# Attention feeding two MLP layers on one core: the opening's loads in another order, and two attention pairs per TensorE visit

## The chip, the core and the metric

The kernel runs on one core of a Trainium2 chip. Its engines each follow their own stream of instructions: TensorE (PE; its weight loads are listed as PEld), VectorE (DVE), ScalarE (ACT), GpSimd (POOL) and SyncE (SP), which here issues every DMA. The metric is the device time of one execution in microseconds (us); less is better.

## The reference

Attention over chunks of 32 tokens, each with 16 tokens before it, 8 after it and 8 memory tokens, for 4 batches of 768 tokens with 8 heads of 64; then two MLP layers on the 3072 tokens (512 to 2048 to 512 features each). All data are float32.

```
for c in range(nc):
    q_c = q[:, :, c_start:c_end]
    k_full = concat([mem_k, k[:, :, l_start:r_end]]);  v_full = concat([mem_v, v[:, :, l_start:r_end]])
    scores = scale * matmul(q_c, k_full.T)
    a = exp(scores - max(scores));  a = a / (sum(a) + 1e-09)
    out[:, :, c_start:c_end] = matmul(a, v_full)
x = out, tokens by features
h = x @ w_in;   x = maximum(0.01 * h, h) @ w_out              # layer 0
h = x @ w_in2;  x = (h * clip(h + 3, 0, 6) / 6) @ w_out2      # layer 1
```

## The kernel before

**Tiling.** The attention is done in 48 pairs of chunks (64 tokens, 8 heads, 96 context columns). A block is 512 tokens, so 8 pairs (`NPB`); there are 6 blocks (`NB`). Each layer goes through its 6 blocks, and a block through 16 steps f (`NF`, 128 hidden features each). A step has a hidden half and an output half (`hidden`, `output`), 12 products of 128x128 by 128x512 each: every operand is split into a high and a low part, and three of the four combinations are multiplied (`mm3`, L567). So the MLPs take 2 x 6 x 16 x 24 = 4608 such products. Between the two halves of a step, ACT applies the activation (L586), ACT writes its high part `gh` (L600) and DVE the low part `gl` (L609).

**Weights.** They arrive as float64 words (`w_load`, L211, 512 KB for one key, a key being one half of one step) in one of four `raw` buffers, and are turned into the high and low parts once per layer by ACT (L217, L223, L251) and DVE (clip L227, shift L231, join L238, add L245, low part L257). The `raw` buffer is free after L257. Layer 0's 32 keys are converted before and during block 0.

**Attention of one pair.** PE computes scores (`a_scores`, L326); in blocks 0 and 1 PE also adds the chunk mask for most pairs (L317), and DVE takes the maximum straight from PSUM (L356), POOL scales it (L367), ACT takes the exponentials, one per head pair with a sum (L402). For the pairs in `SHIFTED`, DVE subtracts the maximum (L375), ACT does one exponential (L387) and DVE adds up (L391). Other pairs are masked on DVE (L336, L362). Then POOL adds a small constant (L414), DVE inverts (L418), POOL normalises (L422). The probabilities are turned by PE (L440, copied by ACT L445) in blocks 0 and 1, by DVE (L432) after that. PE multiplies them with v (`a_values`, L453), and ACT and DVE split the result into the high and low parts of x (L468, L474).

**Order.** The order in which instructions are issued is not that of the loops. `Program` collects every piece of work as a step: engine, estimated length (`TIME`), a due time, the steps that it must follow, and the ring buffers that it takes and frees. `Program.order` then plays a list schedule: whenever an engine is free it takes, of the steps that are ready and whose ring has room, the one due first. Where PE has nothing ready before the opening's last turn, it puts in `keep_warm` (L659), two products of zeros. The instructions are issued in that order for good.

**The opening** is block 0's attention: all 8 pairs must be done before layer 0's first hidden half (due at `BEGIN`). The q and k of its pairs and their v are loaded into buffers of their own. `before = [values_done[x] for x in [pr - 3] if x >= 0]` makes a pair's scores follow the values of the pair three earlier, and a v load follows the q and k load of its pair. **Afterwards** pair pr of blocks 1 to 5 is scored while the block before is in the MLP: PE breaks off its products for a visit (`visit`, `visit_step`), which computes the scores of pair pr and the values of pair pr - 1; the values go into the upper part of the second score bank, `pa1`. q and k of these pairs share one buffer `qk_now`, v one buffer `v_now`. The hidden halves use a ring of two PSUM banks, `ph`.

Of the kernel before, what the change touches and what calls it, by code (L numbers as in the profile page):

```python
# [22 lines left out]
    words=0.67, clip=0.42, shift=0.43, join=0.69, add=0.69, high=0.65, low=0.69, load=0.47,  # L23
    visit=1.2, scores=0.75, masked=0.56, most=0.55, exp=1.65, exp_all=0.52, small=0.15, inverse=0.18, norm=0.83, turn=0.6, turned=0.57, turn4=0.95,
    values=0.85, xh=0.4, xl=0.45, half=1.36, act=0.58, six=0.69, gh=0.6, gl=0.69, done=0.66, warm=0.22,
# [6 lines left out]
STEP_FIRST, STEP_MIXED, STEP = 7.0, 6.6, 5.5  # L32
PAIR_FIRST = 2.1
SHIFTED = (2, 4, 6)


class Program:
# [15 lines left out]
    def order(self, filler):  # L53
# [81 lines left out]
def tile_kernel(  # L135
# [147 lines left out]


    def inputs(pr):
        if pr >= NPB:
            t, vt = qk_t, v_t
        else:
            if pr not in in_t:
                in_t[pr] = sb.tile([P, 2 * 2 * 512], F32, tag="w", name=f"in{pr}", bufs=NF)  # L290
            t, n = in_t[pr], HP * (PT + W)
            t, vt = t[:, :n], t[:W, n:n + HD]
# [3 lines left out]
    def load_qk(pr):  # L296
        nc.sync.dma_start(out=inputs(pr)[0], in_=qk[divmod(pr, PPB)])

    def load_v(pr):
        nc.sync.dma_start(out=inputs(pr)[3], in_=v[divmod(pr, PPB)])  # L300

# [68 lines left out]
    def a_shift(pr):  # L370
        e = sb.tile([P, HP, W], F32, tag="ye", name=f"e{pr}", bufs=4)
        mx = m_t.pop(pr)
        for j in range(2):
# [19 lines left out]

    def a_exp(pr):
        direct = barred_by_pe(pr)
        if direct:
            e_t[pr] = sb.tile([P, HP, W], F32, tag="ye", name=f"e{pr}", bufs=4)
        e, mx = e_t[pr], m_t.pop(pr)
        su = at.tile([P, HP], F32, tag="su", name=f"su{pr}", bufs=4)
        for hp in range(HP):  # L400
            j, m = divmod(hp, HP // 2)
            nc.scalar.activation(  # L402
                out=e[:, hp, :],
                in_=p_t[pr][j][:, m * W:(m + 1) * W] if direct else e[:, hp, :],
                func=AF.Exp,
                scale=SCALE if direct else 1.0,
                bias=mx[:, hp:hp + 1],
                accum_out=su[:, hp:hp + 1],
            )
        s_t[pr] = su  # L410

# [35 lines left out]

    def a_values(pr, pt):
        t, vt = aT_t.pop(pr), inputs(pr)[3]
        for hp in range(HP):  # L450
            for e in range(2):
                c, n = slice(hp * P + e * D, hp * P + (e + 1) * D), e ^ 2 * hp // HP
                nc.tensor.matmul(  # L453
                    pt[e * D:(e + 1) * D, hp * PT:(hp + 1) * PT], vt[:, c], t[:, hp, n * PT:(n + 1) * PT],
                    start=True, stop=True, tile_position=(0, e * D),
                )
# [5 lines left out]
    def a_xh(pr):  # L462
        blk, i = divmod(pr, NPB)
        if (0, blk) not in x_t:
            x_t[0, blk] = tuple(
                sb.tile([P, KD, TB], FR, tag=f"x{c}", name=f"x{c}{blk}", bufs=2) for c in "hl"
            )
        nc.scalar.copy(out=x_t[0, blk][0][:, :, i * PT:(i + 1) * PT], in_=px_t[pr])  # L468

    def a_xl(pr):  # L470
        blk, i = divmod(pr, NPB)
        xh, xl = x_t[0, blk]
        c = slice(i * PT, (i + 1) * PT)
        nc.vector.tensor_sub(out=xl[:, :, c], in0=px_t.pop(pr), in1=xh[:, :, c].bitcast(F32))  # L474
# [3 lines left out]
    def finish(pr, c, t, p):  # L478

        blk = pr // NPB  # L480
        first = pr % NPB == 0
        c = add("ACT", T["xh"], t + 0.8, a_xh, pr, after=[c] + ([] if first else x_ready[blk][:1]),
                takes=[("x", (0, blk))] if first else ())
        d = add("DVE", T["xl"], t + 1.3, a_xl, pr, after=[c], frees=p)
# [12 lines left out]
    def attention(pr, t, turned_by_pe, spread):  # L497

# [4 lines left out]

        qk, vv = [("qk", pr)], [("v", pr)]
        if blk == 0:
            qk = vv = [("w", ("in", pr))]
        hold = [] if blk == 0 else [scored[-3]] if pr == NPB else loaded[-1:]
        a = add("SP", T["load"], due(-5), load_qk, pr, after=hold, takes=qk, nbytes=P * 640 * 4)
        loaded.append(a)
        vl = add("SP", T["load"], due(0), load_v, pr, takes=vv if blk else (), after=[a], nbytes=W * 2048)  # L510
        s = [("py" if blk == 0 else f"pa{j}", ("s", pr, j)) for j in range(2)]
        e = [("ye", ("e", pr))]
        direct = barred_by_pe(pr)
        if blk == 0:
            before = [values_done[x] for x in [pr - 3] if x >= 0]
            c = add("PE", T["scores"] + 0.3 * direct, due(0), a_scores, pr, after=[a] + before + set_up, takes=s)
        else:
            c = visit_step(pr, t, [a], s, qk)
        scored.append(c)
        if direct:  # L520
# [6 lines left out]
            else:  # L527
                c = add("ACT", T["exp"], due(2.0), a_exp, pr, after=[c], takes=e, frees=s)
        else:
            c = add("DVE", T["masked"] + 0.06, due(1.1), a_masked, pr, after=[c] + set_up, takes=e, frees=s)  # L530
            c = add("DVE", T["most"], due(1.7), a_most, pr, after=[c])
            c = add("ACT", T["exp"], due(2.4), a_exp, pr, after=[c])
        c = add("POOL", T["small"], due(4.1), a_sums, pr, after=[c])
# [18 lines left out]
        else:  # L552
            pending[:] = [c, vl, aT + vv]

    def visit_step(pr, t, after=(), takes=(), frees=()):
        if not pending:
            return add("PE", T["scores"], t, visit, pr, after=[*after, opened[-1]], takes=takes, frees=frees)
        p = [*takes] or [("pa1", ("s", pr, 1))]
        c = add("PE", T["visit"], t, visit, pr, after=[*pending[:2], *after], takes=p,
                frees=pending[2] + [*frees])  # L560
        finish(pr - 1, c, t, p[-1:])
        return c
# [148 lines left out]
    for pr in range(NP):  # L711
# [131 lines left out]
```

## Time and profile before

| | |
|---|---|
| median of 3 runs | 1150.18 us (1149.99 to 1150.64) |
| the profiled execution | 1150.69 us, its span 1148.9 us |
| PE busy | 1139.2 us (99%), 6370 matmuls |
| DVE busy | 596.6 us (52%) |
| ACT busy | 467.3 us (41%) |
| POOL busy | 63.1 us (5%) |
| DMA | 78.65 MB, mean 68 GB/s |
| chain that ended last | PE 96%, DVE 2%, ACT 1% |

The profiled execution lies 0.5 us above the median, and 1.8 us of it lie outside the span. Shares are means over very different stages: the opening (to about 40 us), block 0 of layer 0 (to about 142 us) with the conversions, blocks 1 to 4 with visits (to about 533 us), and the rest, where PE does nothing but MLP products. Matmuls are pipelined, so that a PE shown as busy can still be issuing slower than it could; start times tell more than busy time.

### The profile page before, as it was taken

The page shows a single profiled execution, that of the slowest core. Times are in us where ns is not written, and L with a number is a line of the kernel's source. Part 1 is how long each engine was busy: PE and PEld are TensorE (multiplying, and loading weights), DVE is VectorE, ACT ScalarE, POOL GpSimd, SP SyncE. Part 2 cuts the span into 40 slices and gives each one's busy share as a digit, 9 for nine tenths or more (in the row PEclk, how much of TensorE's full clock was granted, in tenths as well). Part 3 has the DMA queues.
Part 4 walks back from the last instruction along what each step waited for, and adds up shares of the span by engine and source line. Part 5 has one row for each costly group of instructions (what it writes and reads, how often), then busy time and mean ns, then how long its engine had stood idle before and what let it go on. Part 6 is the DMA issues. An engine that isn't in the chain of part 4 may idle for free.

```text
span 1148.9 us, 16191 instructions
## 1 busy us (share of the span) xinstructions
PE 1139.2 (99%) x6370; PEld 927.4 (81%) x6370; DVE 596.6 (52%) x1299; ACT 467.3 (41%) x1052; POOL 63.1 (5%) x123
## 2 busy tenths in 40 slices
PE   9999999999999999999999999999999999999998
PEld 6777788888888888888888888888888888888887
DVE  5999985565555555564889723223223223222222
ACT  5888843333333333334777523223223223222222
POOL 3211110010010000100000000000000000000000
PEclk9999999999999999999999999999999999999999
DMA  8456521121111112113554202002002000000001
GB/s 257 142 190 195 184 92 38 55 74 38 56 46 65 56 37 74 57 37 103 179 162 168 92 1 74 1 1 74 1 1 73 1 1 35 3 1 24 14 1 37
DMA packets 31661, 78.65 MB, mean 68 GB/s; under 512 B 3424, under 2 KB 3424, under 8 KB 31584
## 3 DMA queue, kind: packets, MB, share of 16 engines
q1 hardware_dynamic: 31584, 77.61, 20.6%
q8 instruction: 50, 0.82, 0.3%
q14 instruction: 27, 0.22, 0.1%
HBM read 65.01 MB, written 12.58 MB: 68 GB/s over the span
## 4 chain that ended last, share of the span: by engine, by line
PE 96%; DVE 2%; ACT 1%; POOL 0%; issue 0%; DVEq 0%; POOLq 0%
PE py L567 46%; PE ph L567 45%; PE psc L453 2%; PE psc L326 2%; PE warm L659 1%; DVE wa L238 1%; DVE w L257 0%; ACT e L402 0%; PE pt L440 0%; DVE raw L245 0%; DVE wa L231 0%; DVE xl L474 0%; DVE mx L356 0%; DVE wa L227 0%; POOL su L414 0%
## 5 line engine op out<-in xcount | busy, mean ns | idle before, releaser
L567 PE MATMUL ph<-xh,w 128*128 128x512 f32 x768 | 253.1, 391 | 0.0
L567 PE MATMUL ph<-yh,w 128*128 128x512 f32 x768 | 252.0, 389 | 0.0
L567 PE MATMUL py<-gh,w 128*128 128x512 f32 x768 | 242.4, 396 | 0.5 <-DVE w L257 0.5
L567 PE MATMUL py<-w,gh 128*128 128x512 f32 x768 | 236.4, 389 | 0.0
L595 DVE SCALAR_TENSOR_TENSOR ph<-g,ph 128x512 f32<-128x512 f32 x96 | 66.8, 696 | 293.4 <-ACT g L589 293.4
L589 ACT ACTIVATE g<-ph,three 128x512 f32<-128x512 f32 x96 | 66.2, 690 | 297.6 <-PE ph L567 297.6
L567 PEld LDWEIGHTS ph<-xh,w 128*128 128x128 f32 x768 | 144.0, 188 | 30.9 <-DVE w L257 0.4
L567 PEld LDWEIGHTS py<-w,gh 128*128 128x128 f32 x768 | 144.2, 188 | 30.0
L567 PEld LDWEIGHTS ph<-yh,w 128*128 128x128 f32 x768 | 144.2, 188 | 29.8
L567 PEld LDWEIGHTS py<-gh,w 128*128 128x128 f32 x768 | 141.0, 188 | 31.0 <-DVE w L257 1.4
L567 PE MATMUL ph<-xl,w 128*128 128x512 f32 x384 | 149.5, 389 | 0.7 <-DVE xl L474 0.7
L567 PE MATMUL py<-gl,w 128*128 128x512 f32 x384 | 150.0, 391 | 0.0
L567 PE MATMUL py<-w,gl 128*128 128x512 f32 x384 | 149.4, 389 | 0.0
L567 PE MATMUL ph<-yl,w 128*128 128x512 f32 x384 | 149.4, 389 | 0.0
L432 DVE STREAM_TRANSPOSE aT<-e 32x128 f32<-32x128 f32 x384 | 116.0, 302 | 32.8 <-POOL e L422 27.4
L586 ACT ACTIVATE ph<-ph 128x512 f32<-128x512 f32 x96 | 55.9, 583 | 182.3 <-PE ph L567 182.2
L609 DVE TENSOR_TENSOR gl<-ph,gh 128x512 fp32r<-128x512 f32 x96 | 66.2, 690 | 59.6 <-ACT gh L600 58.5
L611 DVE SCALAR_TENSOR_TENSOR gl<-ph,gh 128x512 fp32r<-128x512 f32 x96 | 66.3, 691 | 56.3 <-ACT gh L602 56.1
L567 PEld LDWEIGHTS ph<-xl,w 128*128 128x128 f32 x384 | 72.1, 188 | 16.0 <-DVE xl L474 1.0
L567 PEld LDWEIGHTS py<-gl,w 128*128 128x128 f32 x384 | 72.0, 188 | 15.5
L567 PEld LDWEIGHTS ph<-yl,w 128*128 128x128 f32 x384 | 72.1, 188 | 15.0
L567 PEld LDWEIGHTS py<-w,gl 128*128 128x128 f32 x384 | 72.0, 188 | 15.0
(71 smaller groups left out, 933.3 us busy)
## 6 DMA issues: line engine op xcount, KB each, us to landing
raw<-in_moe_w_in_dram SPq DMA_DIRECT2D x32, 512.0 KB, 3.5
raw<-in_moe_w_out_dram SPq DMA_DIRECT2D x32, 512.0 KB, 3.8
qk_now<-in_qk_dram SPq DMA_DIRECT2D x40, 320.0 KB, 3.2
v_now<-in_v_dram SPq DMA_DIRECT2D x40, 192.0 KB, 2.6
y_dram<-yo SPq DMA_DIRECT2D x24, 256.0 KB, 2.0
yn<-y_dram SPq DMA_DIRECT2D x6, 1024.0 KB, 5.2
out_dram<-oo SPq DMA_DIRECT2D x24, 256.0 KB, 2.7
in<-in_qk_dram SPq DMA_DIRECT2D x8, 320.0 KB, 5.7
```

The costliest lines, as they stand in the source:

```text
L238: nc.vector.scalar_tensor_tensor(out=a, in0=hi, scalar=0xC0000000, in1=a, op0=ALU.bitwise_and, op1=ALU.bitwise_or)
L326: nc.tensor.matmul(pt[j][n * PT:(n + 1) * PT, m * W:(m + 1) * W], qt[r, hp, :], kt[r, hp, :], start=not more, stop=True, tile_position=(e ...
L432: nc.vector.transpose(out=t[c, :, r], in_=e[r, :, c])
L453: nc.tensor.matmul(pt[e * D:(e + 1) * D, hp * PT:(hp + 1) * PT], vt[:, c], t[:, hp, n * PT:(n + 1) * PT], start=True, stop=True, tile_posi ...
L567: nc.tensor.matmul(dst, a, b, start=first and i == 0, stop=last and i == len(terms) - 1)
L586: nc.scalar.activation(out=ph, in_=ph, func=AF.Prelu, alpha=0.01)
L589: nc.scalar.activation(out=g, in_=ph, func=AF.Relu, bias=three, scale=1.0)
L595: nc.vector.scalar_tensor_tensor(out=ph, in0=g, scalar=6.0, in1=ph, op0=ALU.min, op1=ALU.mult)
L609: nc.vector.tensor_sub(out=gl, in0=ph, in1=gh.bitcast(F32))
L611: nc.vector.scalar_tensor_tensor(out=gl, in0=ph, scalar=1.0 / 6.0, in1=gh.bitcast(F32), op0=ALU.mult, op1=ALU.subtract)
L659: nc.tensor.matmul(late["warm"][:, r], idle[:, :P], idle, start=True, stop=True)
```

## The change

In the opening, each pair's v load no longer follows its q and k load, and the first weight keys (f up to 2 of layer 0) are due 35 us instead of 9 us before their use, so that the order of the opening's loads is q and k of pair 0, weight key 0, q and k of pair 1, v of pair 0, and so on. A pair's scores follow the values of the pair five earlier instead of three. Pairs are due 1.9 us apart instead of 2.1. The pairs with a DVE shift are 3 and 5 instead of 2, 4 and 6. The planner counts `keep_warm` at twice its length until 5.5 us, so that fewer are put in at the start. A pair's four exponentials become four steps of the planner instead of one.

From pair 16 on (`doubled`), a visit computes the scores of pairs pr and pr + 1 (pr even) and the values of pairs pr - 2 and pr - 1; the second pair's scores stand in the upper part of the same two score banks, the values of both in a bank of the `ph` ring, and one copy of each kind splits both results. q, k and v of the odd pairs take two of the four `raw` buffers. Layer 1's weight loads wait for the last visit.

```
-SHIFTED = (2, 4, 6)
+PAIR_FIRST = 1.9
+SHIFTED = (3, 5)
+EARLY = 35.0
+COLD = 5.5
...
-                        free_at[e] = now + filler[1]
+                        free_at[e] = now + (filler[1] if now > COLD else 2 * filler[1])
...
-            a = add("SP", T["load"], t - 9, w_load, *key, after=after, takes=raw, nbytes=P * 4096)
+            a = add("SP", T["load"], t - (9 if layer or f > 2 else EARLY), w_load, *key, after=after, takes=raw, nbytes=P * 4096)
...
+    def doubled(pr):
+        return pr >= 2 * NPB
...
+    def raw_buffer(pr, what):
+        t = sb.tile([P, 512, 2], U32, tag="raw", name=f"in{pr}_{what}", bufs=NRAW)
+        in_t.setdefault(pr, []).append(t.rearrange("p c t -> p (c t)").bitcast(F32))
...
-        pt = [bank("py" if pr < NPB else f"pa{j}", f"psc{pr}_{j}") for j in range(2)]
+        if doubled(pr) and pr % 2:
+            pt = [t[:, HP // 2 * W:] for t in p_t[pr - 1]]
+        else:
+            pt = [bank("py" if pr < NPB else f"pa{j}", f"psc{pr}_{j}") for j in range(2)]
...
-    def a_values(pr, pt):
+    def a_values(pr, pt, at=0, every=PT):
...
-        nc.scalar.copy(out=x_t[0, blk][0][:, :, i * PT:(i + 1) * PT], in_=px_t[pr])
+        c = slice((i - 1) * PT if doubled(pr) else i * PT, (i + 1) * PT)
+        nc.scalar.copy(out=x_t[0, blk][0][:, :, c], in_=px_t[pr])
...
     def visit(pr):
         if pr < NP:
             a_scores(pr)
-            pt = p_t[pr][1]
-        else:
-            pt = bank("pa1", f"px{pr}")
-        if pr > NPB:
-            a_values(pr - 1, pt[:, HP // 2 * W:HP // 2 * W + HP * PT])
+            if doubled(pr):
+                a_scores(pr + 1)
+        if pr > 2 * NPB:
+            pt = bank("ph", f"px{pr}")
+            a_values(pr - 2, pt, 0, 2 * PT)
+            a_values(pr - 1, pt, PT, 2 * PT)
+        elif pr > NPB:
+            pt = bank("ph", f"px{pr}") if doubled(pr) else p_t[pr][1][:, HP // 2 * W:]
+            a_values(pr - 1, pt[:, :HP * PT])
...
-        vl = add("SP", T["load"], due(0), load_v, pr, takes=vv if blk else (), after=[a], nbytes=W * 2048)
+        vl = add("SP", T["load"], due(0 if blk else -2.5), load_v, pr, takes=vv if blk else (), after=[a] if blk else (), nbytes=W * 2048)
...
-            before = [values_done[x] for x in [pr - 3] if x >= 0]
+            before = [values_done[x] for x in [pr - 5] if x >= 0]
...
-                c = add("ACT", T["exp"], due(2.0), a_exp, pr, after=[c], takes=e, frees=s)
+                for hp in range(HP):
+                    c = add("ACT", T["exp"], due(2.0 + 0.4 * hp), a_exp, pr, hp, after=[c], takes=() if hp else e,
+                            frees=s if hp == HP - 1 else ())
...
-            attention(pr, block_at[0, blk] - 3.5 - every * (NPB - i), blk == 1, 1.3)
-    visit_step(NP, block_at[0, NB - 1] - 3.5)
+            i -= i % 2 if doubled(pr) else 0
+            attention(pr, block_at[0, blk] - (4.5 if blk == 1 else 6) - every * (NPB - i), blk == 1, 1.6 if blk == 1 else 3.4)
+    attended = visit_step(NP, block_at[0, NB - 1] - 9.0)
...
-    convert(1, lambda f, io: last + (f + 1.4 * io) * STEP - 12)
+    convert(1, lambda f, io: last + (f + 1.4 * io) * STEP - 12, [attended])
```

## Rows read from the trace of the kernel before

**Rows 1.** The chain of work, blocks 1 and 5: start, length, what
```profile
201.95 1.58 PE py L567 x6
...
214.18 1.58 PE py L567 x6
...
533.16 2.72 PE ph L567 x12
```

**Rows 2.** Timeline of PE, one visit, narrow windows: start us, us, instruction, count
```profile
188.76 0.34 PE L326 MATMUL psc<-qk_now 64*64 64x96 f32 x8
...
188.85 0.26 PE L326 MATMUL psc<-qk_now 64*64 64x96 f32 x4
...
189.04 0.69 PE L453 MATMUL psc<-aT,v_now 96*64 96x64 f32 x16
...
189.38 0.35 PE L453 MATMUL psc<-aT,v_now 96*64 96x64 f32 x6
...
189.50 0.23 PE L453 MATMUL psc<-aT,v_now 96*64 96x64 f32 x2
```

**Rows 3.** The chain of work, step 11 of block 0
```profile
118.10 0.61 DVE w L257
...
118.76 2.83 PE py L567 x11
```

**Rows 4.** Windows: stretch, length, busy us of PE, PEld, DVE, ACT, POOL; granted clock; DMA
```profile
100.00:120.00 20.00, 19.38 (x115) 14.91 (x114) 18.96 (x37) 16.75 (x43) 3.22 (x6) 1.00 0.61 183
...
2.00:22.00 20.00, 19.52 (x249) 14.60 (x247) 9.20 (x29) 9.80 (x37) 5.44 (x15) 1.00 1.00 309
```

**Rows 5.** Waits of DVE before 45 us: total us, times, longest
```profile
DVE e L336 <- PE psc L326: 6.2, 1, 6.2
DVE su L418 <- POOL su L414: 2.2, 3, 0.9
DVE xl L474 <- ACT xh L468: 2.0, 1, 2.0
```

**Rows 6.** Timeline of DVE, opening and end of block 0
```profile
17.53 0.42 DVE L227 TENSOR_SCALAR wa<-wa 128x512 f32<-128x512 f32 x1
...
19.27 0.70 DVE L245 CUSTOM_DVE_ANT_0 raw<-raw,wa 128x1024 uint16<-128x1024 uint16 x1
...
20.84 0.62 DVE L375 SCALAR_TENSOR_TENSOR e<-psc,mx 128x192 f32<-128x192 f32 x2
...
23.01 0.54 DVE L391 TENSOR_REDUCE su<-e 128x4 f32<-128x384 f32 x1
...
144.00 0.66 DVE L257 TENSOR_TENSOR w<-raw,w 128x512 fp32r<-128x512 f32 x1
```

**Rows 7.** Timeline of PE, opening
```profile
1.05 6.57 PE L659 MATMUL warm<-idle 128*128 128x256 bf16 x32 [1.05 <-DVE idle L683]
...
7.55 0.56 PE L326 MATMUL psc<-in 64*64 64x96 f32 x16
...
28.99 0.56 PE L326 MATMUL psc<-in 64*64 64x96 f32 x16
...
40.02 0.50 PE L567 MATMUL ph<-xl,w 128*128 128x512 f32 x1 [0.66 <-DVE xl L474]
```

**Rows 8.** DMA issues of q and k (L297) before 30 us, issue to landing
```profile
DMA to landing us min/median/max: 2.9/5.6/7.5
```

**Rows 9.** Timelines of PE and DVE, two steps of block 1
```profile
186.87 0.39 PE L567 MATMUL ph<-xh,w 128*128 128x512 f32 x1
...
188.53 0.69 DVE L609 TENSOR_TENSOR gl<-ph,gh 128x512 fp32r<-128x512 f32 x1 [1.56 <-ACT gh L600]
...
193.66 0.39 PE L567 MATMUL ph<-xh,w 128*128 128x512 f32 x1
...
194.61 2.83 DVE L432 STREAM_TRANSPOSE aT<-e 32x128 f32<-32x128 f32 x9 [0.94 <-POOL e L422]
...
197.47 0.69 DVE L609 TENSOR_TENSOR gl<-ph,gh 128x512 fp32r<-128x512 f32 x1
```

More of the change, by code (lines that the diff above doesn't have):

```diff
@@ L23 @@
     words=0.67, clip=0.42, shift=0.43, join=0.69, add=0.69, high=0.65, low=0.69, load=0.47,
-    visit=1.2, scores=0.75, masked=0.56, most=0.55, exp=1.65, exp_all=0.52, small=0.15, inverse=0.18, norm=0.83, turn=0.6, turned=0.57, turn4=0.95,
+    visit=1.45, visit2=2.1, scores=0.75, masked=0.56, most=0.55, exp=0.37, exp_all=0.52, small=0.15, inverse=0.18, norm=0.83, turn=0.6, turned=0.57, turn4=0.95,
     values=0.85, xh=0.4, xl=0.45, half=1.36, act=0.58, six=0.69, gh=0.6, gl=0.69, done=0.66, warm=0.22,
@@ L290, in inputs @@
                 in_t[pr] = sb.tile([P, 2 * 2 * 512], F32, tag="w", name=f"in{pr}", bufs=NF)
-            t, n = in_t[pr], HP * (PT + W)
-            t, vt = t[:, :n], t[:W, n:n + HD]
+            t, vt = in_t[pr][:, :n], in_t[pr][:W, n:n + HD]
         n = HP * PT
         return t, t[:, :n].rearrange("p (h t) -> p h t", h=HP), t[:, n:].rearrange("p (h w) -> p h w", h=HP), vt
+    def raw_buffer(pr, what):
+        t = sb.tile([P, 512, 2], U32, tag="raw", name=f"in{pr}_{what}", bufs=NRAW)
+        in_t.setdefault(pr, []).append(t.rearrange("p c t -> p (c t)").bitcast(F32))
     def load_qk(pr):
+        if doubled(pr) and pr % 2:
+            raw_buffer(pr, "qk")
         nc.sync.dma_start(out=inputs(pr)[0], in_=qk[divmod(pr, PPB)])
     def load_v(pr):
+        if doubled(pr) and pr % 2:
+            raw_buffer(pr, "v")
+        assert pr in in_t or pr >= NPB
         nc.sync.dma_start(out=inputs(pr)[3], in_=v[divmod(pr, PPB)])
@@ L312, in a_scores @@
         _, qt, kt, _ = inputs(pr)
-        pt = [bank("py" if pr < NPB else f"pa{j}", f"psc{pr}_{j}") for j in range(2)]
+        if doubled(pr) and pr % 2:
+            pt = [t[:, HP // 2 * W:] for t in p_t[pr - 1]]
+        else:
+            pt = [bank("py" if pr < NPB else f"pa{j}", f"psc{pr}_{j}") for j in range(2)]
         more = barred_by_pe(pr)
@@ L392, in a_add_up, with a_exp @@
         s_t[pr] = su
-    def a_exp(pr):
+    def a_exp(pr, hp):
         direct = barred_by_pe(pr)
[L396 to L410, printed above, removed]
+        if hp == 0:
+            if direct:
+                e_t[pr] = sb.tile([P, HP, W], F32, tag="ye", name=f"e{pr}", bufs=4)
+            s_t[pr] = at.tile([P, HP], F32, tag="su", name=f"su{pr}", bufs=4)
+        e, mx, su = e_t[pr], m_t[pr], s_t[pr]
+        j, m = divmod(hp, HP // 2)
+        nc.scalar.activation(
+            out=e[:, hp, :],
+            in_=p_t[pr][j][:, m * W:(m + 1) * W] if direct else e[:, hp, :],
+            func=AF.Exp,
+            scale=SCALE if direct else 1.0,
+            bias=mx[:, hp:hp + 1],
+            accum_out=su[:, hp:hp + 1],
+        )
     def a_sums(pr):
@@ L453, in a_values @@
                 nc.tensor.matmul(
-                    pt[e * D:(e + 1) * D, hp * PT:(hp + 1) * PT], vt[:, c], t[:, hp, n * PT:(n + 1) * PT],
+                    pt[e * D:(e + 1) * D, at + hp * every:at + hp * every + PT], vt[:, c], t[:, hp, n * PT:(n + 1) * PT],
                     start=True, stop=True, tile_position=(0, e * D),
@@ L472, in a_xl @@
         xh, xl = x_t[0, blk]
-        c = slice(i * PT, (i + 1) * PT)
+        c = slice((i - 1) * PT if doubled(pr) else i * PT, (i + 1) * PT)
         nc.vector.tensor_sub(out=xl[:, :, c], in0=px_t.pop(pr), in1=xh[:, :, c].bitcast(F32))
@@ L480, in finish @@
         blk = pr // NPB
-        first = pr % NPB == 0
-        c = add("ACT", T["xh"], t + 0.8, a_xh, pr, after=[c] + ([] if first else x_ready[blk][:1]),
+        first = blk not in x_ready
+        more = 0.25 if doubled(pr) else 0.0
+        c = add("ACT", T["xh"] + more, t + 0.8, a_xh, pr, after=[c] + ([] if first else x_ready[blk][:1]),
                 takes=[("x", (0, blk))] if first else ())
-        d = add("DVE", T["xl"], t + 1.3, a_xl, pr, after=[c], frees=p)
+        d = add("DVE", T["xl"] + more, t + 1.3, a_xl, pr, after=[c], frees=p)
         x_ready.setdefault(blk, []).extend([c, d] if first else [d])
@@ L490, in visit, with attention @@
             a_scores(pr)
-            pt = p_t[pr][1]
-        else:
-            pt = bank("pa1", f"px{pr}")
-        if pr > NPB:
-            a_values(pr - 1, pt[:, HP // 2 * W:HP // 2 * W + HP * PT])
-    def attention(pr, t, turned_by_pe, spread):
+            if doubled(pr):
[7 more added lines that the diff above has]
+            a_values(pr - 1, pt[:, :HP * PT])
+    def attention(pr, t, turned_by_pe, spread, after=None):
         blk = pr // NPB
@@ L504, in attention @@
         qk, vv = [("qk", pr)], [("v", pr)]
+        if doubled(pr) and pr % 2:
+            qk, vv = [("raw", ("qk", pr))], [("raw", ("v", pr))]
         if blk == 0:
             qk = vv = [("w", ("in", pr))]
+        two = doubled(pr)
         hold = [] if blk == 0 else [scored[-3]] if pr == NPB else loaded[-1:]
@@ L514, in attention @@
         if blk == 0:
-            before = [values_done[x] for x in [pr - 3] if x >= 0]
+            before = [values_done[x] for x in [pr - 5] if x >= 0]
             c = add("PE", T["scores"] + 0.3 * direct, due(0), a_scores, pr, after=[a] + before + set_up, takes=s)
+        elif not two:
+            c = visit_step(pr, t, [a], s, qk)
+        elif pr % 2:
+            program.steps[scored[-1]][5].append(a)
+            for k in qk:
+                program.held.setdefault(k, []).append(scored[-1])
+            s = [(k[0], (k[1][0], pr - 1, k[1][2])) for k in s]
+            c = scored[-1]
         else:
@@ L531, in attention @@
             c = add("DVE", T["most"], due(1.7), a_most, pr, after=[c])
-            c = add("ACT", T["exp"], due(2.4), a_exp, pr, after=[c])
+            for hp in range(HP):
+                c = add("ACT", T["exp"], due(2.4 + 0.4 * hp), a_exp, pr, hp, after=[c])
         c = add("POOL", T["small"], due(4.1), a_sums, pr, after=[c])
@@ L557, in visit_step @@
             return add("PE", T["scores"], t, visit, pr, after=[*after, opened[-1]], takes=takes, frees=frees)
[L558 to L561, printed above, removed]
+        p = [("ph", ("x", pr))] if doubled(pr) else takes[-1:]
+        c = add("PE", T["visit2"] if doubled(pr) else T["visit"], t, visit, pr,
+                after=[x for q in pending for x in q[:2]] + [*after], takes=[*takes] + (p if doubled(pr) else []),
+                frees=[k for q in pending for k in q[2]] + [*frees])
+        pending.clear()
+        finish(pr - 1, c, t, p)
         return c
```

7 lines of the change are left out of this document (4 added, 3 removed).

## The prediction

> **What bounds the kernel now.** I read the page first: PE is busy for 99% of the span and makes up 96% of the chain. That says where to look, but not whether PE works or merely waits with an instruction in hand, so next came start times. In the stretch without attention, 12 MLP products take 2.72 us, 0.227 us each [rows 1]; 4608 of them make 1044.5 us. The change leaves that sum alone. About 106 us are left: the opening, the visits, and block 0's waits.
>
> The chain, read block by block, shows the visits. From one visit to the next in blocks 1 to 4 it takes 214.18 - 201.95 = 12.23 us, in which lie two steps, 48 products or 10.88 us by the same row [rows 1]. A visit therefore costs PE 1.35 us, and nothing else is late there.
>
> The chain in block 0 shows another bound. In step 11, DVE ends the low part of a weight key at 118.71 us, and the output half that multiplies with it starts at 118.76 [rows 3]; from 100 to 120 us DVE is busy for 18.96 of 20 us [rows 4]. So in the later steps of block 0, PE is fed key by key by the conversions, without reserve, until the last one ends at 144.66 us [rows 6]. An earlier first product is worth nothing at the end of block 0 unless DVE's conversions come earlier too. That makes the opening a question about DVE's idle time, not PE's.
>
> DVE's waits before 45 us are 6.2 us for the first scores, 2.2 us for POOL and 2.0 us for ACT [rows 5], 10.4 us in all; the rest of that time it works or sets up. This is what the opening can give.
>
> **The change, part by part: two pairs in a visit.** A visit removed does not save all of its 1.35 us, since its products are still made. What a second pair costs behind a first is read inside one visit. Score products start in fours at 188.76 and 188.85 us, 0.09 apart, so four more fours cost 0.36 us at most. Value products start in twos: four of them lie between 189.38 and 189.50, 0.06 per two, so eight twos more cost 0.48 us. What isn't repeated is the change from one tile shape to the next: the last scores start at 188.85, the first values only at 189.04 [rows 2]. A second pair thus costs 0.84 us, and a merge saves 1.35 - 0.84 = 0.51. Before there are visits at pairs 16 to 48, 33 of them; afterwards at the even ones, 17. Sixteen merges save 8.2 us. On top, the scores of pair 17 move from block 1 into the visit at pair 16, which lies in block 0, where PE waits for DVE anyway: 0.4 us. Together **8.6 us**. Bounds: 7 us if half of the second scores' starts cost a shape change after all, 9 if the fours run at the 0.08 that the two-digit times allow.
>
> The Trainium skill (TensorE: Matmul & The Clock Gate, Part 3, The mechanism) says that a weight load overlaps running matmuls only when the row group differs. All value products of a visit use the same 96 rows, so by that rule their loads would not overlap, a second pair would cost as much as a visit of its own, and this part would save nothing. This trace disagrees: the value products start every 0.06 us per two although each runs 0.23 us [rows 2].
>
> The other costs of the visit lie beside PE. One split copy for two pairs replaces two. The odd pairs' q, k, v loads use `raw` buffers that idle in blocks 1 to 4, when layer 0 is converted and layer 1 isn't needed until its own block; the wait of layer 1's loads for the last visit leaves the whole of block 5, some 87 us, for conversions. I cost all that at nothing; the price if it fails is the ring rival below.
>
> **The opening.** Four terms for DVE, up to its last conversion:
>
> - *First scores earlier.* 32 zero products of 256 columns take 6.57 us, 0.205 each [rows 7]; 256 columns are 0.213 us at 1.2 GHz and 0.107 at 2.4. So nearly all of them run at the lower of PE's two levels, although the granted clock of that stretch reads 1.00 [rows 4]. Planned at double length, about half of them remain: they end at 1.05 + 16 x 0.205 = 4.3 us. Pair 0's q and k, first in the queue in both kernels, land 2.9 us after the issue at 0.7 [rows 8], which is earlier. The 16 score products span 0.56 us [rows 7] and at the low level perhaps twice that. The first scores thus end near 5.4 us instead of 7.55 + 0.56 = 8.1, and DVE begins some 2.6 us earlier.
> - *A key in the remaining gaps.* The other 4.2 us of early waits [rows 5] had no conversion to fill them, since weight key 0 was queued behind all q and k. Now it is second. Its four steps up to the add take from 17.53 to 19.97, 2.4 us [rows 6]. I take 2.2 us. Bounds: 0, if the later landing of q and k opens as many new gaps; 4.2 if all close.
> - *One shifted pair less.* 0.62 + 0.54 us of DVE [rows 6], nearly 1.1 net. ACT pays with four exponentials for one, and has room (9.80 us busy of 20 [rows 4]).
> - *Pair 17 ahead of the last conversions.* Its mask and maximum, as much work as those same two rows, now are due before block 0 ends: up to -1.2, I take -0.6. Its q and k may hold one of four `raw` buffers then, which is in the lower bound.
>
> Sum **5.3 us**, between 1 and 9. PE must be able to follow. The loads ahead of pair 7's scores (8 of q and k, some v, three keys) are 5.4 MB; at 309 GB/s [rows 4] that is 17.5 us, so the last lands near 20 us. In the kernel before, pair 7 took from its scores at 28.99 to the split that releases PE at 40.0, 11 us [rows 7]. The first hidden half can then start near 31 instead of 40 us: 9 us, more than 5.3, so DVE binds and PE gives the rest back in waits for L257. Five pairs in flight matter only through this term: without them pair 7 would not start at 20. Four steps for the exponentials move no work.
>
> **Sum.** 1150.7 - 8.6 - 5.3 = 1136.8 for an execution like the profiled one; the median is 0.5 lower, so I say 1136.5.
>
> **Rivals.**
>
> *The opening gives little* (up to 2 us, 1140 to 1144). DVE's gaps may only move, since weight keys now stand in front of pairs in a queue that already runs the DMA engines at a share of 1.00 for 20 us [rows 4]. Or PE stays at 1.2 GHz past 7.6 us, as there is less to keep it busy: the 6.57 us of zero products ran low nearly to their end [rows 7], and each pair's products then take twice as long. The Trainium skill (TensorE: Matmul & The Clock Gate, Part 1) says that the low level is the default and that activity releases it, so by it fewer products can only delay that; no row here has fewer. For it: all of the opening's gain is spent in a stage where I can't see the new order. Against it: DVE's first 6.2 us are idle for one reason only. Chance 0.18.
>
> *The opening gives all that PE can follow*, 9 us (1131 to 1133): if freer ACT order also closes DVE's waits later in block 0. Chance 0.07.
>
> *Merging saves half or nothing* (1140 to 1145.5, which is 1150.7 - 5.3): the second pair pays the shape changes again. Against it stand rows 2. Chance 0.07.
>
> *The two-bank ring turns against it* (slower than before). The values of a visit now take one of the two `ph` banks, so the next hidden half must use the bank of the one that has just ended, and must wait for its `gl`. PE gets there 0.23 + 2.72 = 2.95 us after the last product of that hidden half starts. In block 1, one `gl` ends 188.53 + 0.69 - 186.87 = 2.35 us after it, which fits with 0.6 to spare; the next ends 197.47 + 0.69 - 193.66 = 4.5 us after, because nine transposes were ahead of it [rows 9]. If the transposes fall so in each visit's step, 1.55 us are lost 17 times, 26 us, and the kernel takes 1163. From 0.8 us per visit on it is slower than before. Against it: a visit's own transposes come only after exponentials and normalising, with larger due times (spread 3.4 instead of 1.3), while the bank in question is that of the hidden half cut by the visit. Chance 0.08, of which 0.05 slower.
>
> The forecast itself, 1133 to 1140, has 0.60. Measurements can tell about 0.2%, 2.3 us, from no change. Only the ring rival, and a second mishap beside it, reach there: faster 0.92, same 0.03, slower 0.05. The range 1131.5 to 1143.5 leaves out the worst of the ring and merging cases.
>
> **What would show it.** Visit to visit: 24.46 - 0.51 = 23.95 us for two pairs, blocks 1 to 4 each 2 us shorter. First scores at about 4.4 us, first hidden half near 31, the last L257 of layer 0 near 139.4, and more PE waits for L257 in block 0 than before. Wrong if PE waits for `gl` behind visits, if block 0's last L257 stays near 144, or if the doubled visit takes over 2.4 us.

## The result, and the profile after

The changed kernel takes 1136.04 us (median of 4 runs, 1135.49 to 1137.10), against 1150.34 us for the kernel before on the same chip: a ratio of 0.9879, 95% interval 0.9867 to 0.9891. The forecast was 1136.5. The profiled execution has a span of 1133.69 us and took 1135.49; its counterpart before had 1148.92 and 1150.69. So the two traces differ by 15.2 us, the medians by 14.3.

To find where the time came from, I look for the same instruction in both traces. Three starts are enough: the first hidden half of block 0, of block 1 and of block 5. This is PE's timeline after the change, its rows in the order in which the prediction used [rows 7]: zero products, first scores, the scores of pair 7, the first hidden half and its first `xl` product, and then the first product of block 1. Columns are start us, length us, instruction, count.

```profile
1.04 3.60 PE L701 MATMUL warm<-idle 128*128 128x256 bf16 x16 [1.04 <-DVE idle L725]
...
4.57 0.92 PE L346 MATMUL psc<-in 64*64 64x96 f32 x16
...
21.83 0.56 PE L346 MATMUL psc<-in 64*64 64x96 f32 x16
...
34.21 0.50 PE L609 MATMUL ph<-xl,w 128*128 128x512 f32 x1 [0.38 <-DVE xl L494]
...
136.31 0.39 PE L609 MATMUL ph<-xh,w 128*128 128x512 f32 x1
```

PE is released for the MLP at 34.21 instead of 40.02 us [rows 7], and block 1 begins at 136.31, where the trace of before has 142.26. These 5.95 us are what the opening gave. Block 5 begins at 517.77 instead of 533.00; blocks 1 to 4 thus took 381.46 instead of 390.74 us, 9.28 less, and those are the visits. From block 5 to the end both kernels need 615.92 us. Nothing else changed the span: 5.95 + 9.28 = 15.2.

The visits stand in the chain of waits of block 1 (start, length, what):

```profile
178.04 0.82 PE psc L346 x32
178.86 1.08 PE px L472 x32
179.94 1.59 PE ph L609 x6
...
201.93 0.82 PE psc L346 x32
```

From visit to visit it is 201.93 - 178.04 = 23.89 us, for two pairs; before, two single visits and their steps took 24.46 [rows 1]. The first line is 32 score products in 0.82 us, the second 32 value products in 1.08, without a wait between them or behind them.

Now to block 0, where the prediction had named DVE. These are rows of DVE's timeline after, answering to [rows 6]: the first mask, which waits 3.54 us for the first scores, and the last low part of a layer-0 weight key.

```profile
5.52 0.62 DVE L356 SCALAR_TENSOR_TENSOR e<-psc,masks 128x192 f32<-128x192 f32 x2 [3.54 <-PE psc L346]
...
136.09 0.68 DVE L259 TENSOR_TENSOR w<-raw,w 128x512 fp32r<-128x512 f32 x1
```

Before the change the first mask stood at 8.14 us and waited 6.16:

```profile
8.14 0.62 DVE L336 SCALAR_TENSOR_TENSOR e<-psc,masks 128x192 f32<-128x192 f32 x2 [6.16 <-PE psc L326]
```

The conversions end at 136.77 instead of 144.66 us [rows 6], 7.9 earlier, more than PE gained. Where DVE found them is told by its windows, cut at 34 us and at its last conversion (stretch, length, busy us, granted clock, DMA share, GB/s), of before and then of after:

```profile
0.00:34.00 34.00, 21.80 (x63) 1.00 0.75 233
34.00:144.70 110.70, 104.19 (x211) 1.00 0.57 179
```

```profile
0.00:34.00 34.00, 24.70 (x70) 1.00 0.82 249
34.00:136.80 102.80, 99.03 (x199) 1.00 0.59 183
```

DVE idles 2.9 us less up to 34 us (9.3 instead of 12.2). After that it idles 3.8 instead of 6.5, 2.7 less. Over both stretches its work is 123.74 instead of 125.99, 2.25 less. That is the whole 7.9.

Of the 2.25, 1.54 do not come from the opening. Up to its last low part of layer 0, the trace of before has 33 joins but 32 adds: the clip, shift and join of layer 1's first key already stand there. The changed kernel holds layer 1's loads back until the last visit, and has 32 of each.

```profile
142.18 0.42 DVE L227 TENSOR_SCALAR wa<-wa 128x512 f32<-128x512 f32 x1
...
143.09 0.69 DVE L238 SCALAR_TENSOR_TENSOR wa<-raw,wa 128x512 uint32<-128x512 uint32 x1
```

The idle time of the second stretch has a name: in DVE's waits, the first line of before's list from 34 to 144.7 us is missing from the list of after (what, and for whom; total us, times, longest):

```profile
DVE gl L609 <- ACT gh L600: 2.8, 4, 1.2
DVE xl L474 <- ACT xh L468: 0.6, 2, 0.4
```

```profile
DVE xl L494 <- ACT xh L488: 0.9, 2, 0.4
DVE w L259 <- ACT w L253: 0.3, 1, 0.3
DVE su L437 <- POOL su L433: 0.2, 1, 0.2
```

Early in the opening, by contrast, only part closed. DVE's waits before 45 us, answering to [rows 5]:

```profile
DVE e L356 <- PE psc L346: 3.5, 1, 3.5
DVE su L437 <- POOL su L433: 2.6, 3, 1.3
DVE mx L376 <- PE psc L346: 0.8, 1, 0.8
```

The wait for the first scores shrank by 2.7 us and the 2.0 us for ACT are gone, but the wait for POOL grew from 2.2 to 2.6, and a second one for scores is new.

### The profile page after: what moved, and what is told of

It is laid out like the page before. It is cut to its first block, busy times and chain, and to the rows that moved or that the text cites. A ratio compares the mean times of both kernels' runs of the same rounds, so it can differ in the third digit from the quotient of the medians.

```text
span 1133.7 us, 16067 instructions
## 1 busy us (share of the span) xinstructions
PE 1124.3 (99%) x6326; PEld 922.2 (81%) x6326; DVE 589.5 (52%) x1280; ACT 464.3 (41%) x1043; POOL 60.9 (5%) x123
## 4 chain that ended last, share of the span: by engine, by line
PE 95%; DVE 3%; ACT 1%; POOL 0%; issue 0%; POOLq 0%
PE ph L609 45%; PE py L609 45%; PE px L472 2%; PE psc L346 1%; DVE wa L240 1%; DVE w L259 0%; DVE wa L229 0%; DVE wa L233 0%; DVE raw L247 0%; ACT e L422 0%; PE warm L701 0%; PE pt L459 0%; DVE mx L376 0%; POOL e L441 0%; PE psc L472 0%
## 5 line engine op out<-in xcount | busy, mean ns | idle before, releaser
L609 PE MATMUL py<-gh,w 128*128 128x512 f32 x768 | 239.3, 392 | 0.8 <-DVE w L259 0.8
L609 PEld LDWEIGHTS py<-gl,w 128*128 128x128 f32 x384 | 72.1, 188 | 15.2
L609 PEld LDWEIGHTS py<-w,gl 128*128 128x128 f32 x384 | 72.1, 188 | 15.2
```

The lines of the kernel that those rows point to most:

```text
L609: nc.tensor.matmul(dst, a, b, start=first and i == 0, stop=last and i == len(terms) - 1)
```

## The experiments

Each kernel is the changed one with the edit shown. The theory was that of the prediction: visits and opening each give their share and add up; in block 0, DVE's conversions bind, and PE follows. All times are medians; ratios are to the kernel before, with 95% intervals.

**Each half alone.** The first kernel takes the opening back and keeps the visits:

```
-PAIR_FIRST = 1.9      +PAIR_FIRST = 2.1
-SHIFTED = (3, 5)      +SHIFTED = (2, 4, 6)
-EARLY = 35.0          +EARLY = 9.0
-COLD = 5.5            +COLD = -1.0
-  vl = add("SP", T["load"], due(0 if blk else -2.5), ..., after=[a] if blk else (), ...)
+  vl = add("SP", T["load"], due(0), ..., after=[a], ...)
-  before = [values_done[x] for x in [pr - 5] if x >= 0]
+  before = [values_done[x] for x in [pr - 3] if x >= 0]
```

> The doubled visits as in the change, the opening as before (order of loads, three pairs in flight, pairs 2.1 apart, three shifted pairs, zero products not counted double; the exponentials stay four steps). Theory: both parts act in different stages and add up; the visits alone shorten blocks 1 to 4 by 9.3 us (trace of the changed kernel), block 1 starts near 142, the total is 1141. Rival: pair 17's work ahead of the last conversions holds up block 0, which only the earlier opening paid for: block 1 starts 1 us or more later than 142.3, total 1142 to 1143.

The second keeps the opening and merges no visit:

```
 def doubled(pr):
-    return pr >= 2 * NPB
+    return False
...
-  attention(pr, block_at[0, blk] - (4.5 if blk == 1 else 6) - ..., blk == 1, 1.6 if blk == 1 else 3.4)
+  attention(pr, block_at[0, blk] - 3.5 - ..., blk == 1, 1.3)
-  attended = visit_step(NP, block_at[0, NB - 1] - 9.0)
+  attended = visit_step(NP, block_at[0, NB - 1] - 3.5)
...
-  convert(1, lambda f, io: last + (f + 1.4 * io) * STEP - 12, [attended])
+  convert(1, lambda f, io: last + (f + 1.4 * io) * STEP - 12)
```

> The new opening, with one pair per visit throughout and their due times as before. Theory: block 1 starts near 136.3 as with the whole change, blocks 1 to 4 take 390.7 us as before, total 1144.4. Rival: without pair 17's mask and maximum ahead of the last conversions block 0 ends earlier still, block 1 starts near 135.5, total 1143.5.

Visits alone: 1142.13 us, ratio 0.9929 (0.9914 to 0.9944), 8.2 below before. Opening alone: 1145.13 us, 0.9959 (0.9945 to 0.9973), 5.2 below. Together 13.4 of the 14.3 us, so the halves add up within what the intervals allow; in the traces the spans are 8.6 and 6.0 us shorter, 14.6 of the 15.2. Neither is the old kernel with one part alone, since the planner's lengths (1.45 us for a visit instead of 1.2) and the four steps for the exponentials stay in both. The trace of the visits alone has blocks 1 to 4 at 381.46 us, exactly those of the full change, and that of the opening alone has them at 390.74, those of before: the merge acts there and nowhere else.

What pair 17's work costs block 0 they do not show. With visits alone, block 1 begins at 142.94, 0.7 later than before, but in that trace PE is released at 39.09 instead of 40.02, the last conversion ends at 143.41 instead of 144.66, and the pairs of block 1 have other due times; the 0.7 is the sum of all that. With the new opening the visits make almost no difference to block 1's start (136.31 with them, 136.23 without). This is the start with visits alone, in PE's timeline:

```profile
142.94 0.39 PE L609 MATMUL ph<-xh,w 128*128 128x512 f32 x1
```

They do show how little the end of the last conversion says. The opening alone doesn't hold layer 1's loads back; layer 1's first key is there again, and the last low part of layer 0 ends at 138.36, 1.6 us later than with the whole change. Yet block 1 begins as early. So of the 7.9 us by which DVE's last conversion moved, the opening gave 6.3, and block 1 did not wait for that end.

**What a merge saves.** If the change of tile shape is what isn't repeated, a visit that pays it twice must lose the gain again, with all products the same:

```
-            if doubled(pr):
-                a_scores(pr + 1)
         if pr > 2 * NPB:
             ...
             a_values(pr - 2, pt, 0, 2 * PT)
+        if pr < NP and doubled(pr):
+            a_scores(pr + 1)
+        if pr > 2 * NPB:
             a_values(pr - 1, pt, PT, 2 * PT)
```

> The whole change, but in a doubled visit the scores of the first pair, the values of the first, the scores of the second and the values of the second alternate: the same products in 15 visits with two more changes of tile shape each. Theory: what a merge saves is the shape changes, 0.19 to 0.25 us each against 0.06 to 0.09 between products of one shape; the kernel loses 0.3 us per visit, 4 to 5 us in all, 1140 to 1141. Rival: what a merge saves is leaving the MLP stream half as often, whatever the visit holds; the loss stays under 1 us, 1136 to 1137.

It took 1140.38 us, 0.9915 (0.9900 to 0.9930), 4.3 above the changed kernel. One visit in PE's timeline:

```profile
179.05 0.56 PE L346 MATMUL psc<-qk_now 64*64 64x96 f32 x16
179.54 0.69 PE L472 MATMUL px<-aT,v_now 96*64 96x64 f32 x16
180.15 0.56 PE L346 MATMUL psc<-in_qk 64*64 64x96 f32 x16
180.65 0.69 PE L472 MATMUL px<-aT,in_v 96*64 96x64 f32 x16
181.26 0.50 PE L610 MATMUL ph<-xh,w 128*128 128x512 f32 x1
```

Start to start it is 2.21 us from the first scores to the MLP, where the changed kernel has 179.94 - 178.04 = 1.90. Two more changes of shape thus cost 0.31 us. Only the 15 visits that hold two pairs of each kind alternate: 4.6 us, which is what blocks 1 to 4 lost in the trace (386.06 instead of 381.46 us); the median shows 4.3. By 24.46 - 23.89 a merge saves 0.57 us. The change of shape within a visit is the larger part of it; the other 0.26 us go with breaking off the MLP products half as often, which is what the rival named.

**The parts of the opening, one taken back at a time.** Weight keys late, three pairs in flight, three shifted pairs or none, and the zero products counted at single length:

```
-EARLY = 35.0           +EARLY = 9.0              (keys_late)
-... [pr - 5] ...       +... [pr - 3] ...         (three_flight)
-SHIFTED = (3, 5)       +SHIFTED = (2, 4, 6)      (three_shifted)
-SHIFTED = (3, 5)       +SHIFTED = ()             (none_shifted)
-COLD = 5.5             +COLD = -1.0              (more_zeros)
```

> The whole change, but the first weight keys are due 9 us before use again, so that they stand behind the pairs' q, k and v in the queue. Theory: early keys fill DVE's gaps, 2.2 us; without them the last conversions come that much later and block 1 starts 2 us later, 1138. Rival: PE's first hidden half (34.2 us) and not DVE sets the end of block 0; with keys behind, pair 7's q and k land some 4 us earlier, the first hidden half comes earlier, and the total is 1136 or less.

> The whole change, but a pair's scores follow the values of the pair three earlier again. Theory: DVE's stream hardly changes, but PE's first hidden half falls back to near 39 us, later than DVE needs, and block 1 starts 4 to 5 us later, 1140 to 1141. Rival: the landing of q and k paces the pairs in the new order of loads anyway, about 2.5 us apart, so three in flight are enough: 1136 to 1137.

> The whole change, but pairs 2, 4 and 6 are shifted on DVE instead of 3 and 5. Theory: 1.1 us more of DVE work in the opening delays the conversions and block 1 by as much, 1137. Rival: ACT is as short as DVE in the opening (four exponentials for one), and the end of the opening stays or comes earlier: 1136 or less.

> The whole change with no shifted pair at all: all of the opening's pairs take four exponentials on ACT. One shifted pair more cost 0.8 us by the medians. Theory (DVE's work is what counts): two fewer save 2.2 us of DVE in the opening, and the total falls by 1 to 1.5 us, to 1134.5 to 1135. Rival (DVE and ACT are balanced in the opening, as DVE and PE are in block 0): ACT has 2 x 0.8 us more to do between the pairs, the first hidden half comes 1 to 2 us later than 34.2, and the total is 1136 to 1138.

> The whole change, but the zero products are planned at their single length from the start, so that about 32 stand before the first scores again. Theory: the first scores come near 7.6 instead of 4.6 us and DVE loses 2.6 us at the start, block 1 starts 2 to 3 us later, 1138 to 1139. Rival: the order in which q, k and v land paces the opening, and an earlier pair 0 is worth nothing at its end: 1136 to 1136.5.

| kernel | us | ratio (95%) | above the changed kernel | PE released, us |
|---|---|---|---|---|
| keys_late | 1140.99 | 0.9923 (0.9908 to 0.9938) | 5.0 | 34.95 |
| more_zeros | 1138.09 | 0.9898 (0.9883 to 0.9912) | 2.1 | 36.71 |
| three_flight | 1137.11 | 0.9888 (0.9872 to 0.9905) | 1.1 | 37.68 |
| three_shifted | 1136.84 | 0.9886 (0.9871 to 0.9901) | 0.8 | 35.20 |
| none_shifted | 1136.78 | 0.9882 (0.9866 to 0.9899) | 0.7 | 34.88 |

In the changed kernel PE is released at 34.21. (With three shifted pairs the clock fell in the traced opening, as the last section shows, which is part of its 35.20.) The runs stand on several chips, on which the kernel before took 1149.92 to 1150.34 us, so differences under half a microsecond say nothing. Zeros and three shifted pairs came out as their theory had it. The other three missed it: late keys cost 3 us more than forecast, and three in flight and none shifted come close to the times of their rivals. The rival of three in flight said that landings pace the pairs anyway; but PE is released 3.5 us later there, so that isn't the reason.

The last column hardly orders the times, and that is the finding. With late keys, PE is released only 0.7 us later than in the changed kernel, and yet this kernel loses most of the opening's gain. DVE's windows say why (stretches and columns as above, cut at 16 us), for late keys and then for the changed kernel:

```profile
0.00:16.00 16.00, 7.47 (x31) 1.00 0.92 228
16.00:34.00 18.00, 12.00 (x31) 1.00 0.67 209
```

```profile
0.00:16.00 16.00, 9.14 (x31) 1.00 0.91 285
16.00:34.00 18.00, 15.56 (x40) 1.00 0.73 216
```

By 34 us DVE has done 19.47 us of work instead of 24.70. These 5.2 us are missing later, and the median rises by 5.0. (The traced execution was 2.1 us slower than that median; its block 1 begins at 143.91, 7.6 later, and the last section shows a part of that.) As a price of the prediction's key term this run is too large, though: here the first weight key is issued only at 13.07 us, behind the q, k and v of all eight pairs, while the kernel before issued it at 5.6. It shows that early conversions are worth their length at the end; it does not show that the step gave 2.2 us against before.

Three pairs in flight is the opposite case. Its windows of block 0, from the release of PE to block 1, stand first, those of the changed kernel second (length, then busy us of PE, PEld, DVE, ACT, POOL, granted clock, DMA share, GB/s):

```profile
37.68:137.93 100.25, 100.25 (x686) 80.32 (x686) 95.35 (x192) 82.43 (x197) 13.49 (x22) 1.00 0.58 180
```

```profile
34.20:136.31 102.11, 101.25 (x686) 79.86 (x687) 98.37 (x198) 85.03 (x198) 14.06 (x22) 1.00 0.59 184
```

PE starts 3.5 us later, but DVE had converted in the meantime, and PE runs through block 0 without a gap: the same 686 products in 100.25 instead of 102.11 us. Of 3.5 us late, 1.6 are left at block 1, and 1.1 in the median. So block 0 of the changed kernel contains about 1.9 us in which PE is held back by the conversions and what feeds them.

The two neighbours in shifted pairs are both slightly worse, so ACT's four exponentials for one (none shifted) may begin to cost about as much as DVE's shift (three shifted). Both differ from the changed kernel by less than their intervals; that two is the best number is not shown, only that neither neighbour is better.

**Which engine binds block 0?** Add or remove work on one engine only, and see how much of it arrives. On DVE, the clip (L229, 0.42 us a key) of the 24 keys from f = 4 on is done twice, or left out; a third kernel leaves it out of all of layer 0. On PE, each hidden half of block 0 makes two products more, whose sum the next start overwrites.

```
+  for _ in range(2 if key[0] == 0 and key[1] >= 4 else 1):      (clip_twice)
+  if key[0] or key[1] < 4:                                      (clip_not_late)
+  if key[0]:                                                    (clip_not)
       nc.vector.tensor_scalar(out=a, in0=a, scalar1=LEAST, scalar2=MOST, op0=ALU.max, op1=ALU.min)

+  for _ in range(2 if layer == 0 and blk == 0 and kk == 0 else 0):   (pe_more)
+      nc.tensor.matmul(ph, ah, xh[:, kk, :], start=True, stop=True)
```

> The whole change, with DVE's clip done twice for the 24 keys of layer 0 from step 4 on; the order of instructions is the same otherwise. 24 x 0.42 = 10.1 us more of DVE work in block 0. Theory (DVE binds the end of block 0): block 1 starts 8 to 10 us later, 1144 to 1146. Rival (PE's start binds, DVE has room of several us): 4 us or less, 1140.

> The whole change without DVE's clip for the 24 keys of layer 0 from step 4 on (these weights are then not bounded before they are split); the order is the same otherwise. 10.1 us less DVE work in block 0, none less in the opening. Theory (the forecast: DVE binds and PE, which could start earlier, waits for conversions): those waits go, block 1 starts 3 to 4 us earlier, 1132 to 1133. Rival (PE's first hidden half at 34.2 us binds as much as DVE): only the waits in the trace go, about 1 us, 1135.

> The whole change without DVE's clip for any key of layer 0 (these weights are not bounded before they are split). Against the kernel without the late clips this takes another 8 x 0.42 = 3.4 us from DVE, most of it before the first hidden half. Theory: the opening's end hangs on landings and on the latency of the last pair, so the first hidden half stays near 34 and the total as without the late clips. Rival: DVE paces the last pairs of the opening; the first hidden half comes 1 to 2 us earlier and the total with it, 1133 to 1134.

> The whole change, with two products more in each of block 0's 16 hidden halves (the first product of the half is made three times and the last of them counts). 32 x 0.227 = 7.3 us more of PE work in block 0. Theory (DVE binds the end of block 0, PE waits there): block 1 starts 3 to 4 us later, 1139 to 1140. Rival (PE's start and its work bind as much): 6 to 7 us later, 1142 to 1143.

| kernel | work changed, us | us | ratio (95%) | against the changed kernel | block 1 begins |
|---|---|---|---|---|---|
| clip_twice | DVE +10.1 | 1145.11 | 0.9958 (0.9944 to 0.9973) | +9.1 | 145.65 |
| clip_not_late | DVE -10.1 | 1134.77 | 0.9866 (0.9852 to 0.9881) | -1.3 | 135.38 |
| clip_not | DVE -10.1, and 3.4 less for the first 8 keys | 1134.80 | 0.9869 (0.9852 to 0.9885) | -1.2 | 134.78 |
| pe_more | PE +7.3 (32 products by 0.227) | 1141.03 | 0.9921 (0.9906 to 0.9936) | +5.0 | 141.91 |

DVE's work arrives nearly whole when it grows, as its theory said, and hardly when it shrinks: without late clips the theory, 1132 to 1133, failed, and the rival's 1135 is what came. PE's arrives by two thirds when it grows, between the theory (1139 to 1140) and the rival (1142 to 1143). Three pairs in flight give the scale: 100.25 us is what PE needs for this block when it never waits. With the added products it took 141.91 - 34.23 = 107.68 us, which is 100.25 + 7.3 and 0.1 more; the first 1.7 us of the added work only filled waits. Without any clip PE is released at 33.16, 1.0 us earlier than without the late ones, as the rival there said, but the total is the same, as the theory said. Two engines that both answer to more work, and where less of one brings only 1.3 us, stand in balance: DVE is ahead as the bound by some 1.3 to 1.9 us, and just below it lies PE. Where the 9.1 us went is in the waits of PE from 36 to 146 us with the doubled clip (the changed kernel has 0.8 us for L259 in this block and none for POOL):

```profile
PE pt L460 <- POOL e L442: 3.4, 3, 1.7
PE ph L610 <- DVE w L260: 3.3, 4, 1.5
PE py L610 <- DVE w L260: 1.2, 3, 0.5
```

Not only the keys are late there: the transposes (pt) wait 3.4 us for POOL, though nothing was added to POOL. A slower DVE shows up in PE's list under other names too.

A third engine, ACT, stands in these waits, and no run here adds to it or takes from it. This is the chain behind the changed kernel's one wait for L259, from the end of a hidden half at 119.39 us to the output half that waited (start, length, what):

```profile
119.42 0.59 ACT ph L628
...
121.18 1.30 ACT e L422 x8
...
124.17 0.55 ACT w L253
...
124.75 1.28 DVE w L259
...
126.07 1.43 PE py L609 x5
```

Of these 6.7 us ACT has 5.3 (activation, exponentials and steps of the conversions, one behind the other) and DVE 1.3. Without the late clips the same wait is left, with 0.3 us, behind the same steps of ACT. So what is called DVE's bound here is that of DVE and ACT together, and how much of it is ACT's is not shown.

No kernel here that does all of the work was faster than the changed one.

## Why the prediction was right, step by step

**Visits, 8.6 us: right in mechanism and size.** The prediction read from [rows 2] that a second pair costs 0.36 + 0.48 = 0.84 us. It costs 0.82 - 0.49 = 0.33 for scores and 1.08 - 0.61 = 0.47 for values, 0.80, the single figures by the start times of the alternating visit above. By these figures a merge saves 1.35 - 0.80 = 0.55 instead of 0.51; sixteen make 8.8, and with pair 17's scores (0.33) 9.1 of the 9.28 us of blocks 1 to 4. The Trainium skill's rule (TensorE: Matmul & The Clock Gate, Part 3, The mechanism), that loads overlap running products only in another row group, would have made the second pair's values as dear as a visit's own. By the measured 0.47 us this case disagrees with that rule as it stands. (The same section opens with a second case, a load into the background weight buffer, which would fit; which it was, no run here shows.)

**The ring of two banks: did not happen.** PE's waits after the change contain none for `gl`. This is the list of the whole span (the wait for `idle` is the start):

```profile
PE px L472 <- ACT aT L464: 2.2, 4, 1.1
PE warm L701 <- DVE idle L725: 1.0, 1, 1.0
PE py L609 <- DVE w L259: 0.8, 1, 0.8
PE pt L459 <- POOL e L441: 0.8, 1, 0.8
PE ph L609 <- DVE xl L494: 0.4, 1, 0.4
PE ph L609 <- ACT xh L488: 0.2, 1, 0.2
```

It also answers the prediction's own sign "more PE waits for L257 in block 0 than before": 0.8 us against 0.5, hardly more. That sign failed, as follows.

**The opening, 5.3 us: right sum, wrong steps.** It gave 5.95 us in the trace and 5.2 by medians alone. (The prediction's own terms add up to 1136.3; it gave 1136.5.) Term by term:

- First scores earlier, 2.6 us: 4.57 against a forecast 4.4 us for their start, and DVE's first mask at 5.52 instead of 8.14, 2.6 earlier. Taking back the planner's double length cost 2.1 us. Right. The rival's fear that fewer zero products keep PE at its lower level past 7.6 us did not come true: pair 0's scores at 4.57 took 0.92 us, but pair 1's at 7.42 took 0.56, the length of before [rows 7].
- A key in the remaining gaps, 2.2 us: mis-sized. Of the 10.4 us of early waits, the first scores account for 2.7 less; the other 4.2 became 3.7, the ACT part of it gone and POOL's and PE's parts grown. What made up for it were things the prediction did not count for the forecast: DVE's later waits for ACT's `gh`, 2.8 us to none (the prediction had freer ACT order only in its rival "all that PE can follow"; with the opening alone 0.9 are left), and layer 1's first key, 1.54 us, put off.
- One shifted pair less, 1.1 us, and pair 17's work against it, 0.6: by the lengths of DVE's instructions 1.2 less and 1.2 more, so the two cancel. Three shifted pairs cost 0.8 by the medians, within their intervals.
- DVE's last conversion therefore ended 7.9 us earlier, at 136.77 and not near 139.4; 6.3 of it with the opening alone.

**The step that failed: "The first hidden half can then start near 31 instead of 40 us: 9 us, more than 5.3, so DVE binds and PE gives the rest back".** PE was released at 34.21, only 5.8 earlier. Its terms: the last q and k were forecast to land near 20 us by DMA throughput alone, but they were issued only at 13.09, landed at 21.4, and their scores began at 21.83; from there to the release it took 12.4 us, not the 11 of the kernel before. So PE had no 9 - 5.3 = 3.7 us to give back. Block 0 lasts 102.10 us from release to block 1 after the change, against 102.24 before: its whole length merely moved by PE's 5.8. Both contain about 2 us of waiting by the 100.25 us that PE needs, so DVE, with ACT, still binds, but by 1.3 to 1.9 us. That the time came out as forecast is in this part luck: PE's gain, 3.2 us short, fell to where the forecast had put DVE's.

The reading that DVE alone feeds PE was too narrow as well. [rows 3] are the last links of a chain. In that step of before, PE's products ended at 111.76 us; ACT worked from 111.78 to 115.40, POOL to 116.35, and only then DVE to 118.71:

```profile
114.11 1.29 ACT e L402 x8
...
115.55 0.81 POOL su L414
```

## What to carry to other kernels

Two engines that feed each other need two forecasts: one time for the end of each if it never waited for the other, and the later end counts. It is not the smaller gain that counts: three pairs in flight released PE only 2.3 us earlier than before (37.68 instead of 40.02), and block 1 came 4.3 earlier, because the old block 0 held 2.0 us of waits. Look for a third engine in the chain before naming two. Test it afterwards by adding work to each engine, since adding to one that has reserve costs nothing and taking from one shows how near the next bound is. Where PE interleaves small tiles of different shapes with a dense stream, sort them by shape: in this kernel two changes of shape were 0.31 of the 0.57 us that a merge saved.

## What the runs showed of the hardware

The granted clock fell after PE had been thin. In the kernel with late keys PE waited 1.96 us for POOL and was busy for 0.63 of the 2 us from 88 to 90; the columns are as in the windows above:

```profile
88.00:90.00 2.00, 0.63 (x3) 0.19 (x1) 1.49 (x5) 2.00 (x7) 0.81 (x2) 1.00 0.46 186
90.00:92.00 2.00, 1.41 (x7) 1.28 (x8) 2.00 (x4) 1.46 (x4) 0.54 (x1) 0.85 0.00 0
92.00:94.00 2.00, 2.00 (x6) 1.55 (x5) 2.00 (x5) 1.61 (x3) 0.00 (x0) 0.50 0.93 238
```

A granted clock of 0.50 is the lower level, 1.2 GHz. Seven products then took 94.62 - 91.64 = 2.98 us where 7 x 0.227 = 1.59 is usual: a wait of 2 us cost another 1.4 behind it. That execution took 1143.07 us, 2.1 above the median of its kernel. With three shifted pairs the same happened after two waits for q and k, of 0.93 and 1.55 us: 0.90 us busy from 20 to 22, then a clock of 0.64 and 0.51 in the next two windows. A short wait can so cost more than its length. It need not in every execution: the traced one with three shifted pairs has a mean granted clock of 0.998, its other three have 1.0.

Waits of PE's products for q and k stand neither in the trace of before nor in that of the changed kernel (whose weight loads wait 0.7 us for them), but in some of its variants' traces, such as this one of PE's with three shifted pairs:

```profile
PE psc L346 <- DMA in<-in_qk_dram: 2.5, 2, 1.6
```

The opening now uses q and k about as soon as they land (pair 7's at 21.4, their scores at 21.83), so its time can depend on when they do. The four runs of before lie within 0.65 us of each other, those of the changed kernel within 1.6; that this is the cause was not tried.
